# A fused attention, dense layer and expert kernel: softmax by exponentials with sums, fewer float32 products, a reordered first stage

## The chip, the core and the metric

The kernel runs on one core of a Trainium2 chip. The metric is the time of one execution on the device in microseconds (us). Five engines work side by side, each through its own list of instructions in a fixed order: TensorE (PE: matmuls, with its weight loads as PEld), VectorE (DVE), ScalarE (ACT), GpSimd (POOL) and SyncE (SP), whose list issues most DMAs. An instruction starts when the one before it on its engine is through and the semaphores it waits for are set.

## The reference, cut to what matters

```
# 1. chunked attention: 2 batches, 8 heads, 768 tokens, 64 per head; a chunk of 32 queries sees
#    8 memory keys, 16 tokens to the left, its own 32 and 8 to the right (64 keys in all)
scores = scale * q_c @ k_full.T ;  scores -= max(scores)
a = exp(scores) ;  a = a / (sum(a) + 1e-9) ;  attn = a @ v_full
# 2. dense layer on 1536 tokens of 512: weights in float64, 2048 hidden
h = x @ w_in ;  g = where(h > 0, h, exp(min(h, 0)) - 1) ;  x2 = g @ w_out
# 3. 8 experts, 1536 tokens: pick the best, up to `capacity` rows each
logits = x2 @ w_gate ;  e = argmax ;  gate = softmax(logits)[e]
out = gate * (relu(x2 @ w1[e]) @ w2[e])
```

## The kernel before

The 1536 tokens are cut into six tiles of 256 (a tile is a "pair" of two halves u of 128). The 2048 hidden columns are cut into 16 units f of 128. There are 48 steps; a step is one gemm1 (24 matmuls, L409: 128x256 results, float32r) of two (unit, tile) combinations, the activation, and one gemm2 (L464). Steps 0 to 3 take units 0 to 3 on tiles 0 and 1, steps 4 to 15 take one unit on tiles 0 and 1 each, and then each of tiles 2 to 5 has 8 steps. Step s is followed on TensorE by gemm2 of step s-2.

**First stage (tiles 0 and 1).** Its order is a table of tokens, ORDER (L33): a token such as `sc10` is a piece of work for pair 1, half 0, or, such as `cb3`, for unit 3, or, such as `ma4`, for step 4. Every token issues its instructions at once, so the table is the order on every engine.
- Loads on SP: `lu` a unit (two halves of 512 KB, L315), `lk`, `lq`, `lv` (512, 256, 512 KB, L140).
- Attention of a half: `sc` scores into PSUM (64 matmul records, L169), `tm` row maxima (two reduces, L181), `ts` subtraction of the maxima out of PSUM (two, L187), `ex` one exponential of 128x512 on ScalarE (L195), `to` the sums (L204), plus 1e-9 and reciprocal (L205, L206), `di` the product with it on GpSimd (L211), `fl` four transposes, `fc` their copy out of PSUM (L222), `av` the product with v (L233), `xh` and `xl` the high and low parts of the result, which is gemm1's input (L248 on ScalarE, L252 on VectorE).
- Weights come as 64-bit floats; `ca` (ScalarE, L335), `cb`, `cc`, `cd` (VectorE, L339, L343, L349) make float32 of both halves of a unit. `ch`, `cl` (L358, L362) split the w_in half into a rounded part and a rest, `dh`, `dl` the w_out half.
- `ma` gemm1; `mr` three activations (L423 to L425), `mv` two VectorE instructions (L429, L435) that give the layer's g.
- `mb` gemm2. In steps below NWHOLE = 12 (`whole(s)`), g and w_out stay float32 and one product is made: four matmuls of 128x512 (eight records, `ps<-raw,gt`). In the others `mh` (L439, ScalarE) and `ml` (L443, VectorE) split g, and three float32r products are made: 12 matmuls.
- `pw` is a warm-up: two 128x128 matmuls of the identity into PSUM that nobody reads. There are 36, 35 of them ahead of `ma0`.

**Tiles 2 to 5.** A loop over the steps (L914) emits gemm1 of step s+2, its activation and split (`g1b`, L811), gemm2 of step s, and between them background pieces by a table, PLANS: letter A runs the next piece of the next tile's attention (`attention_pair`, up to its next `yield`), R and S the next piece of a finished tile's routing (`route`, L482), which ends in two scatters to DRAM by GpSimd (L573). Routing needs a matmul of the one-hot choices (L539) that waits for VectorE (`oh`, L534).

The experts' part behind it is not touched by the change.

Of the kernel before, what the change touches and what calls it, by code (L numbers as in the profile page):

```python
# [38 lines left out]
def chunk_attention_elu_mlp_moe(  # L39
# [23 lines left out]
    CH, LEFT, RIGHT, WIN = 32, 16, 8, k.shape[-1]  # L63
    NMEM = WIN - LEFT - CH - RIGHT
    KD = DM // P
    NF = FF // P
    NFE = FE // P
    TT = 256
# [8 lines left out]
    w_in_i = w_in.bitcast(I32)  # L77
    w_out_i = w_out.bitcast(I32)
# [46 lines left out]
    cnti = cp_.tile([1, E], I32, name="cnti")  # L125
    turn = cp_.tile([1, E], I32, name="turn")
    lead = cp_.tile([P, 1], F32, name="lead")
    swap = cp_.tile([1, E], F32, name="swap")

    qs = t4([P, 2, KD, P], F32, "q")  # L130
# [22 lines left out]
    class Pair:  # L153
# [24 lines left out]
        def tm(self, u):  # L178
            self.su[u] = mx = ts_([P, 2, KD], F32, "mx")
            for a, sp in enumerate(self.ps["s", u]):  # L180
                nc.vector.tensor_reduce(out=mx[:, a], in_=sp, axis=AX.X, op=ALU.max)  # L181

        def ts(self, u):
            mx, sp = self.su.pop(u), self.ps.pop(("s", u))
            self.a[u] = t2([P, 2, KD, WIN], F32, "a")
            for a in range(2):
# [7 lines left out]
        def ex(self, u):  # L194
            nc.scalar.activation(self.a[u], self.a[u], AF.Exp, scale=ISC)  # L195

        def to(self, u):
            a = self.a[u].rearrange("p a r w -> p (a r) w")
            if self.t == 0 and u == 0:
                nc.vector.memset(a[0:CH, :, L0:M0], 0.0)  # L200
            if self.t == PPB - 1 and u == 1:
                nc.vector.memset(a[P - CH :, :, R0:WIN], 0.0)
            su = ts_([P, 8], F32, "su")
# [3 lines left out]
            self.su[u] = su  # L207

        def di(self, u, eng=nc.gpsimd):
            a, su = self.a[u].rearrange("p a r w -> p (a r) w"), self.su.pop(u)  # L210
# [35 lines left out]
        def xh(self, u):  # L246
            for i, xp in enumerate(self.ps["x", u]):
                nc.scalar.copy(self.part(u, 0, i), xp)  # L248

        def xl(self, u):  # L250
            for i, xp in enumerate(self.ps.pop(("x", u))):
# [6 lines left out]
    def attention_pair(pi):  # L258
        pp = Pair(pi)
        dve = nc.vector.tensor_copy  # L260

        def finish(u):
            pp.av(u)
            pp.xh(u)
            pp.xl(u)
            if pi + 1 < NP:
                load_v(pi + 1, u)

        def soft(u):
# [24 lines left out]
        yield  # L294
        pp.fl(1)
        pp.fc(1, dve)
        yield
        finish(1)
        yield
# [18 lines left out]
    class Unit:  # L318


        def __init__(self, f):
            self.words = []
            for r in raws.pop(f):
                n = 2 // (1 if r.shape[1] == 1024 else 2)
                self.words.append(r.rearrange("p (a c) t -> p a c t", a=n))

        def lows(self):
            return [r[:, :, :, 0] for r in self.words]
# [4 lines left out]
        def ca(self):  # L333
            for hw in self.highs():
                nc.scalar.activation(f32(hw), f32(hw), AF.Copy, scale=float(2.0**-112))  # L335

        def cb(self):
            for lw in self.lows():
                nc.vector.tensor_scalar(out=lw, in0=lw, scalar1=29, scalar2=None, op0=ALU.logical_shift_right)  # L339

        def cc(self):
            for lw, hw in zip(self.lows(), self.highs()):
                nc.vector.scalar_tensor_tensor(  # L343
                    out=lw, in0=hw, scalar=3, in1=lw, op0=ALU.logical_shift_left, op1=ALU.bitwise_or
                )

        def cd(self):
            for lw, hw in zip(self.lows(), self.highs()):
                nc.vector.scalar_tensor_tensor(  # L349
                    out=lw, in0=hw, scalar=-(1 << 31), in1=lw, op0=ALU.bitwise_and, op1=ALU.bitwise_or  # L350
                )
            self.whole = [f32(w) for lw in self.lows() for w in (lw[:, j, :] for j in range(lw.shape[1]))]

        def main(self, i):

            if not hasattr(self, "un"):
                self.un = t8([P, 2, 2, 512], F32R, "un")
            nc.scalar.copy(self.un[:, i, 0, :], self.whole[i])  # L358
# [9 lines left out]
        def ch(self):  # L368
            self.main(0)

        def cl(self):
            self.rest(0)

        def dh(self):
            self.main(1)

        def dl(self):
            self.rest(1)


    NLEAD, NWHOLE = 4, 12
    steps = []
    for ti in (0, 1):
        for f in range(0, NLEAD, 2):
# [401 lines left out]

    if True:
        make_identity(nc, ident)
        nc.gpsimd.memset(ones, 1.0)
        nc.gpsimd.memset(stri, 1.0)  # L790
        nc.gpsimd.affine_select(
# [18 lines left out]

        def g1b(s):  # L811
            if s < len(steps):
                for o in ("mr", "mv") if whole(s) else ("mr", "mv", "mh", "ml"):
                    do(o + str(s))

        def do(tok):
            op, alt = tok[:2], tok.endswith("*")
            n = tok[2:].rstrip("*+-")
            if op == "pw":
                wp = tps([P, P])  # L820
                for _ in range(2):
                    nc.tensor.matmul(wp, ident, ident, start=True, stop=True)
            elif op == "lz":
                i = int(n) * 2 * P
                nc.sync.dma_start(out=disp[i : i + 2 * P, :].rearrange("(a p) c -> p a c", p=P), in_=blank2(ROW))
# [10 lines left out]
            elif op[0] in "cd" and op != "di":  # L836
                f = int(n)
                if f not in units:
                    units[f] = Unit(f)
                getattr(units[f], op)()  # L840
            elif op[0] == "m":
                s = int(n)
                if op == "ma":
# [7 lines left out]
                elif op == "mh":  # L851
                    pend[s] = elu_h(*pend[s])
                elif op == "ml":
                    gts[s] = elu_l(*pend.pop(s))
                elif op == "mb":
                    gemm2(s)
            else:
# [294 lines left out]
```

## Time and profile before

| what | value |
|---|---|
| median of 3 runs | 568.7 us (567.02, 568.7, 571.47) |
| the profiled execution: time, span | 569.6 us, 567.4 us |
| PE busy | 536.4 us (95%) |
| PEld busy | 455.3 us (80%) |
| DVE busy | 360.7 us (64%), 702 instructions |
| ACT busy | 279.3 us (49%), 451 instructions |
| POOL busy | 48.3 us (9%), 58 instructions |

Read it so: TensorE is busy nearly throughout, but its busy time holds warm-ups and stretches at half clock too; the shares are averages over stages with different limits, so each stage is looked at by itself. In the profile, L numbers are lines of this kernel.

### The profile page before, as it was taken

Reading aid. Unit: us, or ns where it says so; the run is one execution under the profiler, and the core shown is the slowest. Engines: PE = TensorE matmul, PEld = TensorE weight load, DVE = VectorE, ACT = ScalarE, POOL = GpSimd, SP = SyncE. Lnnn points to the kernel's source line nnn. Section 1 sums busy time; section 2 is a strip of 40 time slices with the busy share of each in tenths; the row PEclk is TensorE's granted clock in tenths of the full one; section 3 lists DMA queues with packets and bytes.
Section 4 is the critical chain, followed back from the end, with each engine's and each line's share of the span. In section 5 each row is a group of like instructions: output and inputs, shape, how many; then the busy total and the mean of one; then the engine's idle time right before and its main releaser. Section 6 shows DMA issues by size and latency. Waiting matters only on the chain. (4 is left out here: it accounts for less than half of the span.)

```text
span 567.4 us, 11394 instructions
## 1 busy us (share of the span) xinstructions
PE 536.4 (95%) x4598; PEld 455.3 (80%) x4598; DVE 360.7 (64%) x702; ACT 279.3 (49%) x451; POOL 48.3 (9%) x58
## 2 busy tenths in 40 slices
PE   8699999999998799999989999999999899999996
PEld 8687676678887798898879888777887797799894
DVE  4758979787346535678775787762455774684650
ACT  3357555675442443444254435652555664673440
POOL 0200002000001200100100010120001001001001
PEclk9979999999999899999998999999999999999998
DMA  8979322379932211452002276236651894985400
GB/s 334 355 244 386 133 75 70 116 190 266 368 127 76 82 52 62 162 185 94 21 2 76 94 259 223 99 124 209 256 205 36 304 343 153 327 309 158 157 8 25
DMA packets 34725, 95.95 MB, mean 169 GB/s; under 512 B 3424, under 2 KB 3424, under 8 KB 33888
## 3 DMA queue, kind: packets, MB, share of 16 engines
q1 hardware_dynamic: 32496, 88.68, 45.1%
q0 software_dynamic: 2160, 6.31, 2.9%
q8 instruction: 48, 0.79, 0.6%
q14 instruction: 21, 0.17, 0.1%
HBM read 88.67 MB, written 16.55 MB: 185 GB/s over the span
## 5 line engine op out<-in xcount | busy, mean ns | idle before, releaser
L409 PE MATMUL hp<-xt,un 128*128 128x256 f32 x1152 | 151.8, 290 | 1.0 <-DVE th L435 1.0
L409 PEld LDWEIGHTS hp<-xt,un 128*128 128x128 f32 x1152 | 144.9, 194 | 8.1 <-issue 4.2
L464 PE MATMUL ps<-un,gt 128*128 128x512 f32 x432 | 109.6, 403 | 0.7 <-ACT gt L439 0.7
L464 PEld LDWEIGHTS ps<-un,gt 128*128 128x128 f32 x432 | 79.8, 191 | 20.0 <-ACT e L423 1.2
L651 DVE TENSOR_TENSOR eu<-eraw,eu 128x1024 fp32r<-128x1024 f32 x65 | 77.1, 1222 | 19.3 <-ACT eu L650 19.0
L760 PE MATMUL ps<-eu,ht 128*128 128x512 f32 x336 | 83.1, 399 | 1.1 <-DVE eu L651 0.8
L760 PEld LDWEIGHTS ps<-eu,ht 128*128 128x128 f32 x336 | 61.7, 188 | 15.9 <-DVE eu L651 2.1
L429 DVE SCALAR_TENSOR_TENSOR th<-e,th 128x512 f32<-128x512 f32 x48 | 33.6, 700 | 52.7 <-ACT e L425 47.3
L650 ACT CAST eu<-eraw 128x1024 fp32r<-128x1024 f32 x65 | 65.2, 1046 | 0.8 <-ACT os L766 0.8
L697 PE MATMUL hp<-xd,eu 128*128 128x256 f32 x480 | 59.0, 284 | 2.9 <-DVE eu L651 2.1
L697 PEld LDWEIGHTS hp<-xd,eu 128*128 128x128 f32 x480 | 58.1, 192 | 4.3 <-DVE eu L651 2.5
L439 ACT CAST gt<-th 128x512 fp32r<-128x512 f32 x36 | 22.4, 621 | 62.4 <-DVE th L435 62.4
L423 ACT ACTIVATE e<-hp 128x512 f32<-128x512 f32 x48 | 28.5, 595 | 43.1 <-PE hp L409 39.9
L464 PE MATMUL ps<-raw,gt 128*128 128x512 f32 x96 | 45.5, 616 | 0.3 <-DVE gt L435 0.2
L443 DVE TENSOR_TENSOR gt<-th,gt 128x512 fp32r<-128x512 f32 x36 | 24.9, 693 | 23.8 <-ACT gt L439 23.8
L424 ACT ACTIVATE th<-e 128x512 f32<-128x512 f32 x48 | 30.3, 632 | 10.2 <-PE ps L518 5.5
L683 DVE SCALAR_TENSOR_TENSOR ht<-hp,ht 128x512 fp32r<-128x512 f32 x20 | 13.8, 690 | 33.4 <-ACT ht L682 33.4
L464 PEld LDWEIGHTS ps<-raw,gt 128*128 128x128 f32 x96 | 17.2, 188 | 20.4 <-issue 18.6
L722 PE MATMUL hq<-eu,xd 128*128 128x512 f32 x120 | 30.9, 401 | 1.7 <-PE ps L760 1.0
L766 ACT ACTIVATE os<-ps,xg 128x512 f32<-128x512 f32 x15 | 10.3, 687 | 42.2 <-PE ps L760 23.5
L425 ACT ACTIVATE e<-e 128x512 f32<-128x512 f32 x48 | 30.3, 632 | 1.5
L767 POOL DMA_INDIRECT out_dram<-os,xg x15 | 14.6, 975 | 165.8 <-ACT os L766 165.8
(143 smaller groups left out, 564.3 us busy)
## 6 DMA issues: line engine op xcount, KB each, us to landing
eraw<-in_moe_w_dram SPq DMA_DIRECT2D x32, 1024.0 KB, 8.7
raw<-in_moe_w_in_dram SPq DMA_DIRECT2D x15, 512.0 KB, 6.3
raw<-in_moe_w_out_dram SPq DMA_DIRECT2D x15, 512.0 KB, 7.1
disp<-in_blank_dram SPq DMA_DIRECT2D x12, 514.0 KB, 15.6
kt<-in_k_dram SPq DMA_DIRECT2D x12, 512.0 KB, 5.7
v<-in_v_dram SPq DMA_DIRECT2D x12, 512.0 KB, 4.9
wb<-in_gate_rows_dram SPq DMA_DIRECT2D x6, 1024.0 KB, 4.7
xg<-disp SPq DMA_DIRECT2D x8, 514.0 KB, 4.4
```

The lines of the kernel that those rows point to most:

```text
L409: nc.tensor.matmul(hp[:, j, :], units[f].un[:, 0, wp, kk * P : (kk + 1) * P], xts[ti][:, xp, kk, :], start=(n == 0), stop=(n == 3 * KD - 1),)
L423: nc.scalar.activation(e, hv, AF.Relu, scale=-1.0)
L424: nc.scalar.activation(th, e, AF.Tanh, scale=0.5)
L425: nc.scalar.activation(e, e, AF.Exp, scale=-1.0)
L429: nc.vector.scalar_tensor_tensor(out=th, in0=e, scalar=1.0, in1=th, op0=ALU.add, op1=ALU.mult)
L443: nc.vector.tensor_tensor(out=gt[:, 1, :], in0=th, in1=f32(gt[:, 0, :]), op=ALU.subtract)
L464: nc.tensor.matmul(accs[ti][bl], x, w, start=(f == 0 and n == 0), stop=(f == NF - 1 and n == len(passes) - 1),)
L650: nc.scalar.copy(un[:, 0, :], raw)
L651: lows.tensor_tensor(out=un[:, 1, :], in0=raw, in1=f32(un[:, 0, :]), op=ALU.subtract)
L697: nc.tensor.matmul(hp[:, j, :], w1p(kk, wp, f * P, P), xd[xp][:, kk, :], start=(n == 0), stop=(n == 3 * KD - 1),)
L722: nc.tensor.matmul(hp, self.xd[xp][:, kk, self.b0 * P : (self.b0 + 1) * P], w1p(kk, wp, i * 512, 512), start=(n == 0), stop=(n == 3 * KD - 1),
L760: nc.tensor.matmul(acc, hof(f, gp, j), w2p(f, wp), start=(f == 0 and n == 0), stop=(f == NFE - 1 and n == 2))
```

## The change

1. **Softmax.** Except for the first half of a batch and the last (`edge`: 4 of 12 halves), `ts` now makes minus the scaled maxima (one 128x8 VectorE instruction), and `ex` is eight exponentials of 128x64 straight out of PSUM, each with its own maximum as bias and with the sum of its row as a second result. `to` loses the sum over 128x512. The edge halves go on as before.
2. **float32 second products** in steps 0 to 5 only (NWHOLE 12 to 6); steps 6 to 11 get `mh`, `ml` and three float32r products.
3. **Low halves to GpSimd.** A `+` behind a token puts `cl`, `dl` or `ml` on GpSimd (20 in ORDER), and `g1b` does so for every `ml` of tiles 2 to 5. A `*` puts `ch`, `dh`, `xh` or `di` on VectorE (8 in ORDER).
4. **ORDER** is new throughout: pair 0's q and k are loaded ahead of unit 0; 11 warm-ups are left, all ahead of `ma0`, each one matmul of 256 columns instead of two of 128.
5. **Attention pieces** of later tiles: the first is empty, the others come one piece later; `norm(1)` joins the piece of `fl(0)`, `fc(0)`. Their number stays 8.
6. A method `cz` with `signs` is added to `Unit`; no token calls it. One GpSimd memset of 128x1 fills a constant that only `cz` uses.

```
 ORDER = """
-lu0 ca0 cb0 cc0 cd0 ch0 lk00 lq00 pw pw pw pw pw pw pw pw pw pw pw pw pw pw sc00 tm00
+lq00 lk00 pw pw pw pw sc00 tm00 ts00 ex00 lu0 cb0 to00 ca0 lq01 cc0 lk01 pw pw pw pw sc01
...
+        def edge(self, u):
+            return (self.t, u) in ((0, 0), (PPB - 1, 1))
...
+            else:
+                self.su[u] = nm_ = ts_([P, 2, KD], F32, "nm")
+                nc.vector.tensor_scalar(out=nm_, in0=mx, scalar1=-ISC, scalar2=None, op0=ALU.mult)
+
+        def ex(self, u):
+            if self.edge(u):
+                nc.scalar.activation(self.a[u], self.a[u], AF.Exp, scale=ISC)
+                return
...
             for a in range(2):
-                nc.vector.tensor_tensor(
-                    out=self.a[u][:, a],
-                    in0=sp[a],
-                    in1=mx[:, a].unsqueeze(2).to_broadcast([P, KD, WIN]),
-                    op=ALU.subtract,
-                )
+                for r in range(KD):
+                    nc.scalar.activation(
+                        self.a[u][:, a, r, :], sp[a][:, r, :], AF.Exp,
+                        scale=ISC, bias=nm_[:, a, r : r + 1], accum_out=su[:, a, r : r + 1],
+                    )
...
-            nc.vector.tensor_reduce(out=su, in_=a, axis=AX.X, op=ALU.add)
...
     def attention_pair(pi):
...
+        yield
         soft(0)
         yield
         norm(0)
         yield
         soft(1)
         yield
-        norm(1)
-        yield
         pp.fl(0)
         pp.fc(0)
+        norm(1)
         yield
...
-        def rest(self, i):
-            nc.vector.tensor_tensor(
+        def rest(self, i, eng=nc.vector):
+            eng.tensor_tensor(
...
-    NLEAD, NWHOLE = 4, 12
+    NLEAD, NWHOLE = 4, 6
...
-    def elu_l(th, gt):
-        nc.vector.tensor_tensor(out=gt[:, 1, :], in0=th, in1=f32(gt[:, 0, :]), op=ALU.subtract)
+    def elu_l(th, gt, eng):
+        eng.tensor_tensor(out=gt[:, 1, :], in0=th, in1=f32(gt[:, 0, :]), op=ALU.subtract)
...
         def g1b(s):
             if s < len(steps):
-                for o in ("mr", "mv") if whole(s) else ("mr", "mv", "mh", "ml"):
-                    do(o + str(s))
+                for o in ("mr", "mv", "mh", "ml"):
+                    do(o + str(s) + ("+" if o == "ml" else ""))
...
             if op == "pw":
-                wp = tps([P, P])
-                for _ in range(2):
-                    nc.tensor.matmul(wp, ident, ident, start=True, stop=True)
+                wp = tps([P, 2, P])
+                nc.tensor.matmul(wp, ident, ident.unsqueeze(1).to_broadcast([P, 2, P]), start=True, stop=True)
```

How the lists move at three places. First SP's list from its start: q, kt and v are pair loads, raw is a unit (two halves). Before:

```order
L315 DMA raw_108<-in_moe_w_in_dram 128x1024
L315 DMA raw_108<-in_moe_w_out_dram 128x1024
L140 DMA kt_93<-in_k_dram 128x1024
L140 DMA q_92<-in_q_dram 128x512
L315 DMA raw_201<-in_moe_w_in_dram 128x1024
L315 DMA raw_201<-in_moe_w_out_dram 128x1024
L140 DMA q_92<-in_q_dram 128x512
L140 DMA kt_94<-in_k_dram 128x1024
L140 DMA v_95<-in_v_dram 128x1024
```

Changed:

```order
L141 DMA q_93<-in_q_dram 128x512
L141 DMA kt_94<-in_k_dram 128x1024
L337 DMA raw_161<-in_moe_w_in_dram 128x1024
L337 DMA raw_161<-in_moe_w_out_dram 128x1024
L141 DMA q_93<-in_q_dram 128x512
L141 DMA kt_95<-in_k_dram 128x1024
L337 DMA raw_221<-in_moe_w_in_dram 128x1024
L337 DMA raw_221<-in_moe_w_out_dram 128x1024
L141 DMA kt_94<-in_k_dram 128x1024
```

The first scores' operands are now the first two loads, and unit 0 stands behind them; pair 1's first k comes ahead of pair 0's v.

Second, VectorE's list in tile 2, where the routing of tile 0 forms its one-hot choices (`oh`); th is the activation of a step, gt its split. Before:

```order
L429 SCALAR_TENSOR_TENSOR th_1856<-e_1855,th_1856 128x512
L435 SCALAR_TENSOR_TENSOR th_1856<-hp_1787,th_1856 128x512
L443 TENSOR_TENSOR gt_1861<-th_1856,gt_1861 128x512
L528 MAX rmx_1893<-ps_1884 128x8 x2
L530 MAX_INDEX rix_1894<-rmx_1893,ps_1884 128x8 x2
L531 CAST idf_1895<-rix_1894 128x2
L532 TENSOR_SCALAR nmx_1897<-rmx_1893 128x2
L534 TENSOR_SCALAR oh_1896<-iota_e,idf_1895 128x8 x2
```

Changed:

```order
L474 SCALAR_TENSOR_TENSOR th_1813<-e_1812,th_1813 128x512
L480 SCALAR_TENSOR_TENSOR th_1813<-hp_1787,th_1813 128x512
L573 MAX rmx_1850<-ps_1841 128x8 x2
L575 MAX_INDEX rix_1851<-rmx_1850,ps_1841 128x8 x2
L576 CAST idf_1852<-rix_1851 128x2
L577 TENSOR_SCALAR nmx_1854<-rmx_1850 128x2
L579 TENSOR_SCALAR oh_1853<-iota_e,idf_1852 128x8 x2
```

The split's low half (L443) no longer stands between a step's activation and the routing.

Third, GpSimd's list in tile 2: gt rows are the low halves, a rows the attention's products, disp rows the scatters. Before, from the first scatter:

```order
L573 DMA disp<-x_208_1716,rii_1953 3072x514
L211 TENSOR_TENSOR a_1849<-a_1849,su_2014 128x512
L573 DMA disp<-x_208_1716,rii_1953 3072x514
L211 TENSOR_TENSOR a_2056<-a_2056,su_2112 128x512
L573 DMA disp<-x_209_1720,rii_2169 3072x514 x2
```

Changed:

```order
L618 DMA disp<-x_187_1716,rii_1910 3072x514
L488 TENSOR_TENSOR gt_1928<-th_1923,gt_1928 128x512
L233 TENSOR_TENSOR a_2007<-a_2007,su_2014 128x512
L488 TENSOR_TENSOR gt_2050<-th_2045,gt_2050 128x512
L618 DMA disp<-x_187_1716,rii_1910 3072x514
L233 TENSOR_TENSOR a_2108<-a_2108,su_2109 128x512
L618 DMA disp<-x_188_1720,rii_2175 3072x514
L488 TENSOR_TENSOR gt_2186<-th_2181,gt_2186 128x512
L618 DMA disp<-x_188_1720,rii_2175 3072x514
```

Low halves that gemm2 waits for now stand behind scatters and products on this engine.

## Rows read from the trace of the kernel before

**Rows 1.** Windows: stretch, busy us per engine (instructions), granted clock, DMA share, GB/s.

```profile
20.00:30.00 10.00, 4.98 (x199) 4.21 (x199) 5.52 (x14) 3.39 (x7) 2.08 (x2) 0.92 1.01 396
...
44.50:151.50 107.00, 106.08 (x810) 78.66 (x808) 86.34 (x127) 64.44 (x102) 4.46 (x4) 1.00 0.60 191
151.50:200.60 49.10, 44.20 (x524) 39.79 (x524) 25.79 (x85) 19.35 (x40) 6.23 (x6) 0.97 0.34 121
```

**Rows 2.** Timeline of VectorE at the start: start us, us, instruction, [idle before <-releaser].

```profile
5.96 0.70 DVE L339 TENSOR_SCALAR raw<-raw 128x1024 int32<-128x1024 int32 x1 [5.96 <-DMA raw<-in_moe_w_out_dram]
...
9.67 1.23 DVE L349 SCALAR_TENSOR_TENSOR raw<-raw 128x1024 int32<-128x1024 int32 x1
...
11.47 0.74 DVE L187 TENSOR_TENSOR a<-ps,mx 128x256 f32<-128x256 f32 x2
...
13.58 0.69 DVE L204 TENSOR_REDUCE su<-a 128x8 f32<-128x512 f32 x1
```

**Rows 3.** Timeline of TensorE in the first stage.

```profile
33.76 3.80 PE L409 MATMUL hp<-xt,un 128*128 128x256 f32 x24
...
44.49 6.33 PE L409 MATMUL hp<-xt,un 128*128 128x256 f32 x48
...
78.64 3.76 PE L464 MATMUL ps<-raw,gt 128*128 128x512 f32 x8
...
85.11 3.76 PE L464 MATMUL ps<-raw,gt 128*128 128x512 f32 x8
...
136.57 8.56 PE L464 MATMUL ps<-un,gt 128*128 128x512 f32 x36
144.97 5.90 PE L409 MATMUL hp<-xt,un 128*128 128x256 f32 x48
151.53 3.14 PE L409 MATMUL hp<-xt,un 128*128 128x256 f32 x24 [0.66 <-DVE th L435]
```

**Rows 4.** Groups by line and shape: busy us, mean ns of one.

```profile
L429 DVE SCALAR_TENSOR_TENSOR th<-e,th 128x512 f32<-128x512 f32 x48 | 33.6, 700 | 52.7 <-ACT e L425 47.3 <-PE ps L169 3.8 <-issue 1.3
...
L252 DVE TENSOR_TENSOR xt<-ps,xt 128x256 fp32r<-128x256 f32 x24 | 9.0, 416 | 8.8 <-ACT xt L248 8.7
...
L195 ACT ACTIVATE a<-a 128x512 f32<-128x512 f32 x12 | 7.6, 631 | 27.0 <-DVE a L187 27.0
```

**Rows 5.** Timeline of ScalarE: two small exponentials with sums, then the next activation.

```profile
171.20 0.27 ACT L535 ACTIVATE ex<-ps,nmx 128x8 f32<-128x8 f32 x1 [1.04 <-DVE nmx L532]
...
171.70 0.59 ACT L423 ACTIVATE e<-hp 128x512 f32<-128x512 f32 x1
```

**Rows 6.** Timeline of TensorE in tiles 2 and 4.

```profile
171.42 0.18 PE L539 MATMUL ps<-oh,stri 128*128 128x8 bf16 x1 [1.37 <-DVE oh L534]
...
189.27 1.23 PE L233 MATMUL ps<-at,v 64*64 64x32 f32 x64 [1.64 <-ACT at L222]
191.75 0.65 PE L217 MATMUL ps<-ident,a 128*128 128x128 f32 x4 [1.25 <-POOL a L211]
192.16 4.59 PE L464 MATMUL ps<-un,gt 128*128 128x512 f32 x12
...
296.54 1.14 PE L233 MATMUL ps<-at,v 64*64 64x32 f32 x64 [1.77 <-DVE at L222]
```

**Rows 7.** Timeline of VectorE in tile 2: the split's low half.

```profile
169.70 0.69 DVE L443 TENSOR_TENSOR gt<-th,gt 128x512 fp32r<-128x512 f32 x1 [0.69 <-ACT gt L439]
```

**Rows 8.** Timeline: GpSimd's product beside VectorE, and where VectorE reads PSUM.

```profile
84.98 1.83 POOL L211 TENSOR_TENSOR a<-a,su 128x512 f32<-128x512 f32 x1 [57.35 <-DVE su L206]
...
85.95 1.95 DVE L349 SCALAR_TENSOR_TENSOR raw<-raw 128x1024 int32<-128x1024 int32 x1
...
182.90 1.03 POOL L211 TENSOR_TENSOR a<-a,su 128x512 f32<-128x512 f32 x1 [7.55 <-DVE su L206]
```

**Rows 9.** Timeline at the end of tile 5.

```profile
360.52 1.28 POOL L573 DMA_INDIRECT disp<-x,rii  x1 [3.25 <-DMA disp<-x,rii]
...
362.45 3.32 PE L464 MATMUL ps<-un,gt 128*128 128x512 f32 x12 [0.67 <-ACT gt L439]
```

More of the change, by code (lines that the diff above doesn't have):

```diff
@@ L127, in chunk_attention_elu_mlp_moe @@
     lead = cp_.tile([P, 1], F32, name="lead")
+    nought = cp_.tile([P, 1], F32, name="nought")
     swap = cp_.tile([1, E], F32, name="swap")
@@ L181, in tm @@
                 nc.vector.tensor_reduce(out=mx[:, a], in_=sp, axis=AX.X, op=ALU.max)
+        def edge(self, u):
+            return (self.t, u) in ((0, 0), (PPB - 1, 1))
         def ts(self, u):
-            mx, sp = self.su.pop(u), self.ps.pop(("s", u))
+            mx = self.su.pop(u)
+            if self.edge(u):
+                sp = self.ps.pop(("s", u))
+                self.a[u] = t2([P, 2, KD, WIN], F32, "a")
+                for a in range(2):
+                    nc.vector.tensor_tensor(
+                        out=self.a[u][:, a],
+                        in0=sp[a],
+                        in1=mx[:, a].unsqueeze(2).to_broadcast([P, KD, WIN]),
+                        op=ALU.subtract,
+                    )
+            else:
+                self.su[u] = nm_ = ts_([P, 2, KD], F32, "nm")
+                nc.vector.tensor_scalar(out=nm_, in0=mx, scalar1=-ISC, scalar2=None, op0=ALU.mult)
@@ L194, in ex @@
[L194 to L204 removed]
+                for r in range(KD):
+                    nc.scalar.activation(
+                        self.a[u][:, a, r, :], sp[a][:, r, :], AF.Exp,
+                        scale=ISC, bias=nm_[:, a, r : r + 1], accum_out=su[:, a, r : r + 1],
+                    )
@@ new lines, in to @@
+        def to(self, u):
+            if self.edge(u):
+                a = self.a[u].rearrange("p a r w -> p (a r) w")
+                if u == 0:
+                    nc.vector.memset(a[0:CH, :, L0:M0], 0.0)
+                else:
+                    nc.vector.memset(a[P - CH :, :, R0:WIN], 0.0)
+                self.su[u] = ts_([P, 2, KD], F32, "su")
+                nc.vector.tensor_reduce(out=self.su[u].rearrange("p a r -> p (a r)"), in_=a, axis=AX.X, op=ALU.add)
+            su = self.su[u]
@@ L244, in part, with xh @@
             return x.rearrange("p (g i) x -> p i g x", i=2)[:, i]
-        def xh(self, u):
+        def xh(self, u, cp=nc.scalar.copy):
             for i, xp in enumerate(self.ps["x", u]):
-                nc.scalar.copy(self.part(u, 0, i), xp)
+                cp(self.part(u, 0, i), xp)
         def xl(self, u):
@@ L335, in ca, with cz @@
                 nc.scalar.activation(f32(hw), f32(hw), AF.Copy, scale=float(2.0**-112))
-        def cb(self):
-            for lw in self.lows():
-                nc.vector.tensor_scalar(out=lw, in0=lw, scalar1=29, scalar2=None, op0=ALU.logical_shift_right)
+        def cz(self):
+            x = t4([P, 1024], F32, "sign")
+            self.signs = []
+            for i, hw in enumerate(self.highs()):
+                n = hw.shape[1]
+                to = x[:, i * 512 : i * 512 + n * 512].rearrange("p (a c) -> p a c", a=n)
+                nc.scalar.activation(to, f32(hw), AF.Identity, scale=float(2.0**-100), bias=nought)
+                self.signs.append(to.bitcast(I32))
+        def cb(self):
+            for i, lw in enumerate(self.lows()):
+                if self.signs:
+                    nc.vector.scalar_tensor_tensor(
+                        out=lw, in0=lw, scalar=29, in1=self.signs[i],
+                        op0=ALU.logical_shift_right, op1=ALU.bitwise_or,
+                    )
+                else:
+                    nc.vector.tensor_scalar(out=lw, in0=lw, scalar1=29, scalar2=None, op0=ALU.logical_shift_right)
         def cc(self):
@@ L366, in rest, with ch, cl, dh @@
                 self.words = self.whole = None
[L368 to L378, printed above, removed]
-    NLEAD, NWHOLE = 4, 12
+        def ch(self, **kw):
+            self.main(0, **kw)
+        def cl(self, **kw):
+            self.rest(0, **kw)
+        def dh(self, **kw):
+            self.main(1, **kw)
+        def dl(self, **kw):
+            self.rest(1, **kw)
+    NLEAD, NWHOLE = 4, 6
     steps = []
@@ L839, in do @@
                     units[f] = Unit(f)
-                getattr(units[f], op)()
+                kw = {}
+                if alt:
+                    kw = {"cp": nc.vector.tensor_copy}
+                elif tok.endswith("+"):
+                    kw = {"eng": nc.gpsimd}
+                getattr(units[f], op)(**kw)
             elif op[0] == "m":
```

25 lines of the change are left out of this document (17 added, 8 removed).

## The prediction, made before the changed kernel ran

> **What bounds the kernel now.** I read the busy shares first: TensorE is busy 95%, so time can only be won by giving it less to do, by letting it start its real work earlier, or by closing its waits. The windows by stage say which of these is open where [rows 1]. From 44.5 to 151.5 us TensorE is busy 106.1 of 107.0 us at full clock (1.00): there only less work helps, and VectorE, busy 86 us of the same stretch, is not far behind. From 151.5 to 200.6 us (tile 2) it is busy 44.2 of 49.1. Before 44.5 its busy time is largely warm-ups; the DMAs run flat out (share 1.01 at 396 GB/s between 20 and 30 us) and the clock is 0.92 there. The timeline of TensorE gives the landmarks of the first stage [rows 3]: the first gemm1 begins at 33.8 us, that of step 2 at about 47.7 (44.5 plus half of the 6.3 of two), tile 2's first at 151.5. So I price four things: when step 2's gemm1 can begin, what lies between it and tile 2, the waits in tiles 2 to 5, and the end of tile 5. What follows the dense layer is the same program, and I carry it over unchanged.
>
> **Second products.** One step with float32 takes 6.47 us from gemm2 to gemm2 (78.64 to 85.11). With three float32r products it is 2.80 for gemm2 (36 matmuls, 136.57 to 144.97, three steps) and 2.95 for gemm1 (48 in 5.90, two steps), together 5.75 [rows 3]. Difference 0.72, six steps: **-4.3 us** of a TensorE that is full there. For it, six more `mh` and `ml` run: 3 to 4 us on ScalarE, which is busy 64 of 107, and on GpSimd or VectorE.
>
> **The early start.** From row 1 of VectorE: 1 MB, the first load, has landed at 5.96 us [rows 2]. At 396 GB/s the 0.75 MB of q and k that now lead land about 0.7 us sooner, near 5.2, and scores need some 0.9: VectorE can start attention at 6.1. From there I count VectorE's list up to the last input of step 2's gemm1 (pair 1's last `xl`), with row durations less the 0.05 to 0.08 by which instructions of one engine overlap in the timeline. Conversion of a unit: 0.62 + 1.17 + 1.17 = 2.96, five units, 14.8 [rows 2]. Row maxima of five halves, 0.70 each for a pair (the subtraction pair took 0.74): 3.5. One edge subtraction 0.70 and three small ones of 0.18: 1.2. Sums: one in the old way 1.2 (0.69 plus small ones), three new ones 0.36 each: 2.3. Four `xl` of two, 0.68: 2.7 each 0.42 less the overlap [rows 4]. One activation pair 1.4 0.70 each [rows 4]. Moved to VectorE by a `*`: 2.0. Sum 27.9. Walking the list against ScalarE, GpSimd and the landings (512 KB each 1.3 us at that rate, units 0 to 3 by 24 us), I find VectorE idle 4.9 us, nearly all while eight exponentials run. So step 2's gemm1 begins at 6.1 + 27.9 + 4.9 = 38.9, say 39.7 with TensorE's own list: **-8.0 us** against 47.7. The 24 warm-ups that go lay ahead of that point and cost nothing by themselves; what they kept up, the clock, is rival 2.
>
> The eight exponentials themselves: two small ones with sums took 0.50 us from start to start [rows 5], 0.25 each for 8 elements; from 0.27 at 8 to 0.63 at 512 elements [rows 4] 56 more cost some 0.04, an estimate, at most 0.1. So 2.3 to 2.8 us a half instead of 0.63, while VectorE loses 0.74 + 0.69 and gains 0.18. I take 2.5. In the dense part this runs beside ScalarE's idle time; on the chain of a half it adds about 0.5 us.
>
> **From step 2 to tile 2** it was 103.8 us. Off go 4.3, and 0.8 for one half's scores that now come earlier. Against it stands a collision. The product on GpSimd took 1.03 us where VectorE read PSUM, but 1.83 beside VectorE's conversions, and a conversion 1.95 instead of 1.23 [rows 2, 8]. Twenty low halves and five products now run there in the first stage. I take +2.0 us of waits for it (bounds: 0 if VectorE keeps ahead, 6.6 as in rival 1). **-3.1.**
>
> The Trainium skill has a rule on this (SBUF — State Buffer, Who interferes with whom): a VectorE instruction with two SBUF inputs and a GpSimd instruction that reads SBUF use one shared port pair as an exclusive lock, and the second to issue waits until the first is through. By that rule a low half moved to GpSimd beside a busy VectorE gives VectorE back nothing; the two lengthened rows agree with it, and rival 1 is what would follow.
>
> **Tile 2.** TensorE waited 1.37 for the one-hot choices, 1.64 for `fc`'s copy, 1.25 for the product, and the gemm2 behind them took 4.59 instead of 2.80 [rows 3, 6]: the clock had fallen to its half level, 1.2 GHz, after these waits. Together 6.1. The choices were late because VectorE stood 0.69 us waiting for ScalarE's rounding and then made the low half, 0.69, ahead of them [rows 7]; both are gone. In my walk the new pieces put two gemm1, a gemm2 and the second half's scores between `di` and `fl` of the first half, and `fc` is late by 0.5 only, behind eight exponentials. **-5.6**; bounds: 0 if the exponentials hold up `fc` and the clock as before, -6.1.
>
> **Tiles 3 to 5.** The pattern repeats in tile 4: a second wait of 1.4 for the choices, one of 1.77 for a copy on VectorE [rows 6], a second slow matmul group behind it. VectorE now reaches both 1.3 us sooner, so the first goes and the other shrinks; I take **-3.3**, bounds 0 and -5. The `ml` of these steps has time: ready some 5.5 us after its gemm1, wanted two gemm2 and two gemm1 later, 11.5. Only the last two steps have no gemm1 behind them: there TensorE already waited 0.67 for the split [rows 9], and GpSimd needs 1.03 to 1.83 instead of 0.69: **+1.0** (0.3 to 2).
>
> **Sum.** -8.0 - 3.1 - 5.6 - 3.3 + 1.0 = -19.0, from the profiled execution's 569.6 us: 550.6. That execution lies 0.9 above the median of 568.7, so I forecast **550 us** for the median.
>
> **Rival 1: VectorE becomes the pace.** From step 2's gemm1 to that of step 7 my count gives VectorE 34.3 us and TensorE 32.8, so there is no room. About nine GpSimd instructions fall in this stretch; each holds VectorE up by 0.72 (1.95 less 1.23) [rows 2, 8]: 6.6 us instead of the 2.0 allowed, and about 2 of tile 4's gain go the same way. Against it: some of these meet VectorE at PSUM reads or waits. Time 550 + 4.6 + 2 = 556.6. Chance 0.18.
>
> **Rival 2: the early start is lost to the clock.** With 11 warm-ups TensorE is mostly idle up to step 0's gemm1, at about 24 us; even with 35 the clock was 0.92, and the first gemm1 took 3.80 us [rows 1, 3]. If the half level lasts through three gemm1 and a gemm2 (some 13 us at full), and half of that is hidden by VectorE's list, step 2 begins 6 to 7 us later: 557. Chance 0.12.
>
> **Rival 3: GpSimd's list paces tiles 2 to 5, slower than before.** A low half stands behind scatters; one waited 3.25 us for the scatter before it and took 1.28 [rows 9]. A tile has 8 low halves, 2 products and 2 to 4 scatters: at 1.83, 1.83 and 4.5 us that is 27 to 36 us of the 46 that eight steps take. If instructions there cost half as much again it passes 46; then each of 32 steps waits, at 0.85 us 27 us in all: 577. Against it: 10 us of room, and two steps of lead. Chance 0.06.
>
> **Chances and range.** The forecast has 0.64. The range must take in rivals 1 and 2 and the bounds: below, all of the collision's 2.0, another 0.5 in tile 2 and 1.7 in tile 4, and some more if step 2 starts with less idle time on VectorE: 540. Above, rival 2 with part of rival 1: 561. Less than 2 in 10 is left out. A change of 1% (5.7 us) is about what a measurement of this kernel can tell from none. Faster by more: 0.88 (the forecast and rivals 1 and 2, less their overlap beyond 563); within 1%: 0.05; slower: 0.07 (rival 3 and a little).
>
> **What would show it.** Step 0's gemm1 near 24 to 26 us and step 2's near 40; tile 2's first gemm1 near 140 instead of 151.5; gemm2 of steps 6 to 11 as 12 matmuls in 2.8 us; exponentials of 128x64 every 0.3 us; no wait on `oh` in tiles 2 and 4, and no slow matmuls behind it; tile 2 some 43 us long. Wrong would be: TensorE waiting for VectorE's `th` or `gt` in steps 3 to 8 (rival 1), a granted clock near half up to 40 us with gemm1 of 5 to 6 us (rival 2), or TensorE waiting for GpSimd's `gt` in tiles 2 to 5 (rival 3).

## The result, and the profile after

The changed kernel took **552.1 us** (median of 548.2 to 555.1) beside 568.7 before: ratio 0.970, 95% interval 0.963 to 0.977. On a second chip the same program took 555.8 (553.7 to 559.4) beside 569.7: 0.977 (0.970 to 0.983). So it is 14 to 17 us faster; I had forecast 550 within 540 to 561.

The profiled execution took 555.1 us (span 553.4; before 569.6 and 567.4). Its windows by stage, in the columns of [rows 1]:

```profile
10.00:20.00 10.00, 7.02 (x201) 5.60 (x202) 8.38 (x15) 6.27 (x23) 4.40 (x4) 0.59 1.03 416
20.00:30.00 10.00, 8.79 (x227) 7.12 (x225) 8.71 (x17) 8.66 (x39) 3.76 (x3) 0.90 1.02 397
30.00:42.91 12.91, 11.90 (x164) 9.78 (x165) 10.38 (x19) 7.02 (x13) 1.67 (x2) 0.74 1.03 415
42.91:142.00 99.09, 97.83 (x746) 79.55 (x745) 82.71 (x112) 64.22 (x115) 25.97 (x20) 1.00 0.64 207
142.00:187.14 45.14, 43.54 (x527) 39.49 (x525) 22.07 (x77) 21.00 (x54) 14.25 (x12) 0.96 0.22 71
...
345.55:553.40 207.85, 191.11 (x1115) 163.65 (x1113) 106.42 (x140) 101.44 (x142) 20.05 (x20) 0.99 0.52 184
```

Step 2's gemm1 begins at 42.9 us (before 47.8), tile 2's first at 142.0 (151.5), the experts' part at 345.6 (365.6). (What the prediction and this text call tile 2's first gemm1 is that of step 18, the first that the loop emits; steps 16 and 17, also of tile 2, run ahead of it in both kernels, so the comparison holds.) The dense part ends 20.1 us earlier; the experts' part, which the change does not touch, took 207.9 us instead of 201.8 and gives 6 of that back. Its window before:

```profile
365.61:567.40 201.79, 189.22 (x1115) 162.43 (x1113) 106.70 (x140) 101.46 (x142) 19.16 (x18) 0.99 0.54 188
```

TensorE's timeline of the changed kernel, to be read beside [rows 3] (up to 104.13 us) and [rows 6, 9] (the rest):

```profile
24.34 0.39 PE L454 MATMUL hp<-xt,un 128*128 128x256 f32 x1
24.89 3.02 PE L454 MATMUL hp<-xt,un 128*128 128x256 f32 x23 [0.16 <-DVE xt L274]
...
31.01 0.63 PE L239 MATMUL ps<-ident,a 128*128 128x128 f32 x4 [1.72 <-DVE a L233]
...
34.97 4.93 PE L454 MATMUL hp<-xt,un 128*128 128x256 f32 x24
39.74 3.76 PE L509 MATMUL ps<-raw,gt 128*128 128x512 f32 x8
42.91 3.45 PE L454 MATMUL hp<-xt,un 128*128 128x256 f32 x24
...
98.46 2.96 PE L509 MATMUL ps<-un,gt 128*128 128x512 f32 x12
101.26 3.03 PE L454 MATMUL hp<-xt,un 128*128 128x256 f32 x24
104.13 2.94 PE L509 MATMUL ps<-un,gt 128*128 128x512 f32 x12
...
177.09 1.14 PE L255 MATMUL ps<-at,v 64*64 64x32 f32 x64 [1.55 <-ACT at L244]
178.27 0.66 PE L239 MATMUL ps<-ident,a 128*128 128x128 f32 x4
178.69 4.60 PE L509 MATMUL ps<-un,gt 128*128 128x512 f32 x12
...
250.22 0.17 PE L587 MATMUL ps<-oh,stri 128*128 128x8 bf16 x1 [0.88 <-DVE oh L579]
...
343.12 2.60 PE L509 MATMUL ps<-un,gt 128*128 128x512 f32 x10 [0.63 <-POOL gt L488]
```

In tile 2 one wait is left, for `fc`'s copy, and behind it the slow gemm2 (4.60 instead of 2.96). Of the choices' waits one of 0.88 in tile 4 remains. The copy is late because of what stands ahead of it on ScalarE:

```profile
172.65 1.29 POOL L488 TENSOR_TENSOR gt<-th,gt 128x512 fp32r<-128x512 f32 x1 [2.26 <-ACT gt L484]
...
172.76 1.21 DVE L202 TENSOR_SCALAR nm<-mx 128x8 f32<-128x8 f32 x1
...
174.09 0.31 ACT L213 ACTIVATE a<-ps,nm 128x64 f32<-128x64 f32 x1 [1.58 <-DVE nm L202]
174.30 0.19 ACT L213 ACTIVATION_READ_ACCUMULATOR a<-ps,nm 128x1 f32 x1
174.39 0.31 ACT L213 ACTIVATE a<-ps,nm 128x64 f32<-128x64 f32 x1
...
176.41 0.62 ACT L244 COPY at<-ps 128x512 f32<-128x512 f32 x1
```

These are lines of GpSimd, VectorE and ScalarE: the eight exponentials of the second half start every 0.29 us (2.3 us in all; the forecast said 2.3 to 2.8) and the first half's copy stands behind them; and they began late, since the 8-element scaling of the maxima took 1.21 us beside a low half on GpSimd.

### The profile page after: what moved, and what is told of

Same layout as the page of the kernel before. It is cut to its first block, busy times and chain, and to the rows that moved or that the text cites. A ratio compares the mean times of both kernels' runs of the same rounds, so it can differ in the third digit from the quotient of the medians.

```text
span 553.4 us, 11372 instructions
## 1 busy us (share of the span) xinstructions
PE 523.3 (95%) x4500; PEld 448.5 (81%) x4500; DVE 348.1 (63%) x651; ACT 293.5 (53%) x569; POOL 120.1 (22%) x108
## 5 line engine op out<-in xcount | busy, mean ns | idle before, releaser
L509 PE MATMUL ps<-un,gt 128*128 128x512 f32 x504 | 127.2, 401 | 1.4 <-POOL gt L488 1.3
L509 PEld LDWEIGHTS ps<-un,gt 128*128 128x128 f32 x504 | 92.7, 191 | 22.5 <-POOL gt L488 2.4
L805 PE MATMUL ps<-eu,ht 128*128 128x512 f32 x336 | 84.7, 404 | 6.2 <-ACT eu L695 3.4
L805 PEld LDWEIGHTS ps<-eu,ht 128*128 128x128 f32 x336 | 62.9, 191 | 21.5 <-issue 5.7
L488 POOL TENSOR_TENSOR gt<-th,gt 128x512 fp32r<-128x512 f32 x33 | 45.8, 1388 | 127.9 <-ACT gt L484 127.8
L484 ACT CAST gt<-th 128x512 fp32r<-128x512 f32 x42 | 26.1, 620 | 73.3 <-DVE th L480 73.3
L407 POOL TENSOR_TENSOR un<-raw,un 128x512 fp32r<-128x512 f32 x16 | 23.6, 1481 | 56.7 <-ACT un L403 40.5
L480 DVE SCALAR_TENSOR_TENSOR th<-hp,th 128x512 f32<-128x512 f32 x42 | 29.1, 692 | 4.0 <-DVE th L474 0.5
```

The lines of the kernel that those rows point to most:

```text
L480: nc.vector.scalar_tensor_tensor(out=to, in0=hv, scalar=0.0, in1=th0, op0=ALU.max, op1=ALU.subtract)
L488: eng.tensor_tensor(out=gt[:, 1, :], in0=th, in1=f32(gt[:, 0, :]), op=ALU.subtract)
L509: nc.tensor.matmul(accs[ti][bl], x, w, start=(f == 0 and n == 0), stop=(f == NF - 1 and n == len(passes) - 1),)
L805: nc.tensor.matmul(acc, hof(f, gp, j), w2p(f, wp), start=(f == 0 and n == 0), stop=(f == NFE - 1 and n == 2))
```

## The experiments

Beside each median, "start" is tile 2's first gemm1 in the trace, "tiles" the time from there to the experts' part, "experts" the rest. Before: 151.5, 214.1, 201.8. Changed: 142.0, 203.5, 207.9. These three come from one profiled execution of each kernel, which can lie some us from the median.

**The six steps' products alone, first try** (kernel before):

```
-NLEAD, NWHOLE = 4, 12
+NLEAD, NWHOLE = 4, 6
-... mv6 ... mb6 dh6 ... dl6        (and 7 to 11)
+... mv6 mh6 ml6 ... dh6 dl6 mb6
```

> The kernel before with one part of the change: steps 6 to 11 make three float32r products (NWHOLE 6), their rounding and low half on ScalarE and VectorE. My step: six steps at 0.72 us less on a TensorE that is full there, -4.3 us, so about 564.4, and tile 2's first gemm1 at about 147.2 instead of 151.5. Rival (VectorE is nearly as full): its six more low halves (3.7 us) eat it, -1 to -2 us, 567, with TensorE waiting for gt or un.

610.4 us, ratio 1.072 (1.070 to 1.074). I had put `dh6` straight ahead of `mb6`, and so behind the next step's activations in ScalarE's list, which wait for that step's gemm1: gemm2 could no longer run beside them, and TensorE waited 4.8 to 7.4 us in front of three gemm2. That says nothing on the products.

**The table of before in the changed kernel, with the same misplaced tokens:**

> The changed kernel with the first stage's table of before (with the rounding and low half of steps 6 to 11 added), all else as changed. If the early start and the reordering are worth what the change's trace shows (-9.5 us at tile 2's first gemm1, of which 4.3 are the products), the first gemm1 of tile 2 comes at 147 and the whole at about 557 (552 + 5). Rival: the lighter softmax by itself brings most of the early start (VectorE has 1.2 us less per half): step 2's gemm1 already 2 to 3 us earlier, the whole at 554. In tiles 2 to 5 both expect the gains of the change (some 10 us from tile 2's first gemm1 to the end of step 47), since these parts are kept.

596.0 us, 1.045 (1.041 to 1.049), spoiled in the same steps. Two things can be read outside of them: step 2's gemm1 came at 48.3, so the lighter softmax alone brings nothing of the early start (that rival falls); and tiles took 203.3 us, so the gain there does not hang on the first stage.

**The products alone, mended:** each `dh dl` pair of units 6 to 11 stands behind a step's `ml` or a unit's `cl`, ahead of the next step's activations.

> As the first try of this part (six more steps with three float32r products in the kernel before), but with the w_out halves of units 6 to 11 rounded and split ahead of the next step's activations on ScalarE and VectorE, not behind them: in the first try gemm2 of steps 6 to 11 waited up to 7.4 us for un, because its rounding stood behind the next step's gemm1 in ScalarE's list. With that mended my step should hold: six times 0.72 less, -4.3 us, 565, tile 2's first gemm1 at 147.2. Rival: VectorE has no room for six more low halves and six earlier ones (7.4 us): -2 to +3 us, with waits for un or th in steps 8 to 12.

580.3 us, 1.021 (1.016 to 1.027). The rival came true, and worse than I had put it. Up to step 7 nothing is lost (-1.1 us); then TensorE waits for VectorE and ScalarE, three of its waits:

```profile
89.45 4.03 PE L409 MATMUL hp<-xt,un 128*128 128x256 f32 x22 [2.26 <-DVE un L362]
...
100.75 0.49 PE L464 MATMUL ps<-un,gt 128*128 128x512 f32 x1 [1.20 <-ACT un L358]
...
106.44 4.83 PE L464 MATMUL ps<-un,gt 128*128 128x512 f32 x12 [2.08 <-ACT gt L439]
```

Between 84 and 110 us VectorE is busy 23.0 of 26, and in the kernel before it was busy 23.1 in the same stretch, where TensorE did not wait at all: it had little room for more. Tile 2 starts at 157.3, 5.8 us later than before. In the old table the six steps cost time in both placings that were tried; a better one may exist.

**All but the table:** the changed kernel with this mended table.

> The changed kernel with the first stage's table of before, with the mended places for the six steps' halves; all else as changed. If the reordering is worth what the traces showed (5.2 of the 9.5 us by which tile 2 starts earlier), tile 2's first gemm1 comes at 147 and the whole is 5 us above the changed kernel, 557 to 561. From tile 2's first gemm1 to step 47 it takes 190.5 us as in the changed kernel (200.7 before). Rival (order and products only work together, the old table leaves VectorE no room): tile 2 starts at 150 or later, the whole 564 or more.

562.6 us, 0.988 (0.983 to 0.994). Start 156.3, tiles 201.8. As to tile 2's start the rival came true again: the new table, with its marks, is worth 12 to 14 us at tile 2's start (142.0, and 144.2 in the second trace of the changed kernel), not 5.

**The first stage's low halves on VectorE:**

```
-... cl1+ ... cl0+ ... cl2+ ...
+... cl1  ... cl0  ... cl2  ...     (20 tokens; the expectation counted 18)
```

> The changed kernel with the 18 low halves that the first stage's table puts on GpSimd moved to VectorE (0.6 us each, 11 us more on an engine that is busy 82.7 of 99.1 us). Relief theory: VectorE becomes late, TensorE waits for un and th in steps 2 to 10, tile 2 starts 4 to 8 us later, 557 to 560. Lock theory (each low half on GpSimd holds VectorE up by about 0.7 us as it is): within 1.5 us of the change, 552, and VectorE's conversions come down from 1.32 to 1.23 us.

560.4 us, 0.987 (0.983 to 0.990). The relief theory came true: tile 2 starts at 151.25, 9.3 us later than in the first trace of the changed kernel and 7.1 later than in the second. That is still 5 us ahead of the old table (156.3), so the new order gives something without its `+` marks too. Step 2's gemm1 comes at 47.1 instead of 42.9, and a later step waits 4.0:

```profile
28.07 4.88 PE L454 MATMUL hp<-xt,un 128*128 128x256 f32 x22 [3.35 <-DVE un L407]
...
38.76 0.78 PE L255 MATMUL ps<-at,v 64*64 64x32 f32 x37 [2.18 <-issue]
...
127.23 4.31 PE L454 MATMUL hp<-xt,un 128*128 128x256 f32 x22 [4.00 <-DVE un L407]
```

`issue` means that TensorE waited for nothing that the profile shows; that line is no work of VectorE, see the run with the moved code. What VectorE paid shows in the windows up to tile 2's first gemm1, this kernel first (VectorE is the third busy time), then the changed one:

```profile
0.00:151.25 151.25, 133.60 (x1414) 108.40 (x1415) 116.61 (x187) 88.61 (x190) 8.35 (x19) 0.93 0.70 244
```

```profile
0.00:142.00 142.00, 131.95 (x1414) 106.73 (x1415) 113.11 (x167) 89.24 (x190) 37.26 (x39) 0.94 0.74 260
```

Twenty instructions of 0.7 us, 14 us, left VectorE, and it is busy only 3.5 us less: the others grew (the scaling of the maxima from 0.18 to 0.63 us, mean of four; `cb` from 0.75 to 0.82; `cd` from 1.22 to 1.32). The Trainium skill (SBUF — State Buffer, Who interferes with whom) says that a VectorE instruction with two SBUF inputs contends with a GpSimd instruction that reads SBUF, under an exclusive lock; `cd`, which has two, agrees. The scaling and `cb` have one SBUF input and grew too. If each low half on GpSimd held VectorE up for as long as it would have taken there, the move would return nothing; measured, a quarter came back. The time gained at tile 2's start is larger than that: with the low halves on VectorE, TensorE waits for them (`un`, 3.35 and 4.00 us above).

**Low halves of g in tiles 2 to 5 on VectorE:** `do(o + str(s))` in `g1b`, without the `"+"` for `ml`.

> The changed kernel with the low halves of g in tiles 2 to 5 on VectorE as before. My theory: they put the one-hot choices late; TensorE's wait for oh (1.4 us each in tiles 2 and 4) comes back, and with it a slow gemm2 or two; less 0.6 us in the last two steps: +2 to +5 us, about 555. Rival 1 (the shared port makes VectorE pay for GpSimd's low halves anyway): 0 within 1 us. Rival 2: GpSimd's low halves cost more than they give, -1 to -3 us.

559.0 us, 0.982 (0.980 to 0.983). My theory was right in kind and too small: tiles 210.8, 7.2 us more. The wait for `oh` is back in tile 4 (2.24 instead of 0.88) and not in tile 2; the first wait below is in the changed kernel too (1.55):

```profile
178.31 1.13 PE L255 MATMUL ps<-at,v 64*64 64x32 f32 x64 [1.67 <-ACT at L244]
...
253.75 0.17 PE L584 MATMUL ps<-oh,stri 128*128 128x8 bf16 x1 [2.24 <-DVE oh L579]
286.27 1.14 PE L255 MATMUL ps<-at,v 64*64 64x32 f32 x64 [0.96 <-DVE at L244]
308.90 0.17 PE L651 MATMUL ps<-cum,ones 128*128 128x8 bf16 x1 [1.31 <-DVE cum L596]
```

**The pieces of attention as before** (the `yield` ahead of `soft(0)` gone, `norm(1)` ahead of `fl(0)` as a piece of its own):

> The changed kernel with the pieces of attention in tiles 2 to 5 cut as before (softmax of the first half starts one place earlier, transposes and copy of the first half after the second half's product). My theory: the wait for GpSimd's product in front of the transposes comes back in tiles 2 and 4, 1.25 us each, with a slow gemm2 behind the one of tile 2: +2 to +4 us. Rival (only the order of low halves and choices matters there): within 1 us.

563.2 us, 0.988 (0.983 to 0.994), 7.3 us above the changed kernel on this chip, and so more than forecast. In the trace tiles are 213.4, 9.9 us more; that execution took 568.8, 5.6 above the median, so 9.9 may be too much. In tile 2:

```profile
181.34 1.14 PE L255 MATMUL ps<-at,v 64*64 64x32 f32 x64 [3.55 <-ACT at L244]
184.52 1.11 PE L239 MATMUL ps<-ident,a 128*128 128x128 f32 x4 [2.04 <-POOL a L233]
```

Eight exponentials in the old pieces hold up the copy by 3.55. So GpSimd's low halves (7.2) and the new pieces (9.9) do not add up: in these traces the low halves alone keep 0.7 of the 10.5, the pieces alone 3.3. Both were run with the eight exponentials, so the old pieces with the old softmax are not shown.

**The softmax of before** (`edge` true for every half, the zeroing only where `edge` was true):

> The changed kernel with the softmax of before in all halves (two subtractions, one exponential, one sum over 128x512), order and all else kept. My count: VectorE gets 1.2 us more for each of the three light halves ahead of step 2's gemm1, but gets the exponentials 1.7 us sooner each; the two cancel: step 2's gemm1 within 1 us, the whole +1 to +2 us, 553 to 554. In tile 2 the wait for the copy of the first half (1.55 us) goes, since the eight exponentials no longer stand ahead of it, and VectorE's 1.2 us more comes back as a wait for oh. Rival (VectorE's load decides, as where the first stage's low halves went back to it: +7.6 us for 11 us more on VectorE): +3 to +5 us.

550.2 us (549.1 to 553.9), 0.966 (0.961 to 0.970), beside 555.8 of the changed kernel on this chip. Start 143.9, 1.9 later than in the first trace of the changed kernel and 0.3 earlier than in the second; tiles 200.3, 3.2 and 2.6 us less, nearly all of it in tile 2; the experts' part took 208.0. I had missed the sign: the eight exponentials do not pay here. Of the 5.6 us between the medians the traces show 2.5. Tile 2 without them:

```profile
177.33 1.14 PE L255 MATMUL ps<-at,v 64*64 64x32 f32 x64
178.44 0.66 PE L239 MATMUL ps<-ident,a 128*128 128x128 f32 x4
178.85 3.05 PE L509 MATMUL ps<-un,gt 128*128 128x512 f32 x12
```

No wait, and no slow gemm2. VectorE's longer subtractions and sums cost nothing there.

**The changed kernel again:**

> The changed kernel as it is, as the measure for the others of this chip: 552 us (548 to 555). In its first trace TensorE stood still at two places of the experts' part, 3.2 us (546 matmuls behind its start) and 1.9 us (921 behind), and that part took 207.9 us instead of 201.8. If the place is set by the program, both stalls are there again within 0.5 us; if by what the DMAs happen to do, other places and other sizes.

555.8 us. Experts 207.6. Both stalls are at the same matmuls as in the first trace, and smaller by 0.6 and 0.5 us. The first block below is of this run, the second of the first trace:

```profile
448.28 7.32 PE L805 MATMUL ps<-eu,ht 128*128 128x512 f32 x24 [2.59 <-ACT eu L695]
...
515.78 4.22 PE L805 MATMUL ps<-eu,ht 128*128 128x512 f32 x17 [1.37 <-issue]
```

```profile
446.76 5.83 PE L805 MATMUL ps<-eu,ht 128*128 128x512 f32 x24 [3.23 <-ACT eu L695]
...
512.96 5.77 PE L805 MATMUL ps<-eu,ht 128*128 128x512 f32 x17 [1.91 <-issue]
```

The profile names ScalarE's `eu` for the first, but on the weight loads the same idle time reads `[3.40 <-issue]`: nothing it knows was late. The DMA queues in that stretch (443.5 to 446.9 us; packets, MB, share of 16 engines) hold a transfer of another kind:

```profile
q1 hardware_dynamic: 522, 1.28, 100.0%
q8 instruction: 1, 0.02, 1.7%
```

**The code moved:** 32 matmuls more ahead of the first scores.

> The changed kernel with 32 matmuls of 16 columns whose result nobody reads, put where TensorE waits for the first k (8.1 to 10.3 us), so that everything behind keeps its work and stands 64 instructions later in TensorE's list. The trace has transfers of 16 KB on a queue of kind 'instruction', one for each 250 or so instructions of TensorE, and one of them lies inside each of the two stalls of the experts' part (at 444.2 and 510.5 us). If TensorE stood still there for its own instructions, the stalls leave their places (546 and 921 matmuls behind the start of that part) and the part's length changes by 1 to 6 us, while step 2 to tile 5 stay within 1 us. Rival (an input was late there): the 3.2 us stall stays at its place.

558.8 us, 0.982 (0.977 to 0.988). My filler was too dear: each matmul is two records with a weight load each (so 128 instructions, not 64), and they took 10.6 us, far more than the 2.2 in which TensorE waits there:

```profile
5.15 10.56 PE L871 MATMUL ps<-ident 128*128 128x16 f32 x64
15.64 1.19 PE L170 MATMUL ps<-kt,q 64*32 64x64 f32 x64
```

Scores are 10 us late and tile 2 starts 7.7 us late. But tiles took 203.5 as in the changed kernel, and experts **203.4** instead of 207.6 to 207.9: neither stall is at its place, and the longest idle times left are two of 1.6 us at other matmuls. The same work, moved in TensorE's list, lost them.

Moving the code also moved everything in time, but the other traces settle that. Count TensorE's matmul records ahead of the experts' part. Where there are as many as in the changed kernel (its two traces, the two with low halves on VectorE, the pieces of before), idle time stands at the 546th matmul of that part (1.2 to 3.2 us) and at the 921st or 922nd (0.9 to 2.0), and the part takes 205.8 to 210.8, whether it begins at 345.6 or at 356.2 us. Where there are 24 to 98 more (the kernel before, both runs with the table of before, this run and the two below), neither place stalls, and the part takes 201.8 to 203.7. The two runs of the products alone have 122 more, with their weight loads 244 instructions, and both stalls are back, at the 546th and at the 924th or 925th (parts of 205.4 and 208.8). The softmax of before is the one that does not fit: as many matmuls as the changed kernel, but five more waits in TensorE's list, and idle times at the 602nd and 918th.

**A version put together from the runs, and the same with half the filler:** softmax of before, `ml` of steps 46 and 47 on VectorE, and in place of the four warm-ups ahead of `sc01` 64 (or 32) matmuls of 8 columns in bfloat16.

> A version put together from the runs: the changed kernel with the softmax of before (550.2 beside 555.8 on one chip), the low halves of the last two steps on VectorE, and 64 matmuls of 8 columns in place of four warm-ups (112 instructions more in TensorE's list, near the 128 of the run with the moved code, in which the experts' part took 203.4 us instead of 207.6 to 208). Expected: -0.6 us for the last two steps, -4 us for the experts' part if the stalls leave, 545 to 546. Rival 1: the stalls only change places, 549. Rival 2: without these warm-ups the clock keeps TensorE back up to step 2's gemm1, 1 to 3 us later.

> The same with 32 of the small matmuls (48 instructions more instead of 112). If the stalls of the experts' part come from where TensorE's blocks of instructions end, this version differs from the other in that part by 1 to 5 us, either way, and their dense parts agree within 1 us. If they come from inputs or from the DMAs' load, both take the same.

**545.1 us** (544.9 to 545.2), 0.958 (0.954 to 0.963), and 547.3 (546.8 to 551.3), 0.964 (0.958 to 0.970). The first beats both kernels. Start 141.5 and 141.2, tiles 200.0 and 200.7, experts 201.9 and 203.4: their dense parts agree, the experts' parts differ by 1.5, and the second kernel has a stall of 2.33 at a new place (403.6 us) with an instruction transfer at 401.3. Rival 2 of the first expectation fell: with the small matmuls in place of four warm-ups step 2's gemm1 came at 41.0, earlier than 42.9.

## Why the prediction was right, and where it was not

The forecast case came true, but its terms moved against each other, so that the total came out within 2 us is in part luck. Term by term in the traces (first, and second execution of the changed kernel):

- Early start: forecast -8.0, measured -4.9 and -5.1. VectorE's list was about right: its last input was done at 40.5 us, forecast 38.9. What failed is "39.7 with TensorE's own list": TensorE had waited 1.72 us for VectorE's product (31.01), and behind that wait its granted clock was 0.66 and then 0.57, the lower level (1.2 GHz) for most of the time. The two products with v took 3.4 us there and gemm1 of step 1 4.8, together some 3 us more than the same groups take at full clock later in this trace; so gemm2 of step 0 ran only from 39.74 to 42.9. That is a piece of rival 2, about half its price.
- Step 2 to tile 2: forecast -3.1, measured -4.7 and -2.3. The rows of a step came as priced (2.80 and 2.87 us from start to start at 98.46, 101.26 and 104.13, 5.7 a step). But "six steps at 0.72" was put down as a gain of its own, and by itself it was none: in the old table, as I placed them, the same six steps cost 5.8 us. The saving came only with the room that the new table makes. I had the sum about right with wrong parts.
- The collision on GpSimd and VectorE, +2.0: from step 2 to tile 2 TensorE's waits for GpSimd's `gt` and `un` sum to 1.1 us (0.65 and 0.48). Rival 1's lengthening is real, but the low halves on GpSimd are worth 7 to 9 us all the same.
- Tiles 2 to 5 with the end: forecast -7.9 (5.6 and 3.3 off, 1.0 on), measured -10.5 and -11.2. By tiles, in the first trace: -3.9 in tile 2, nothing in tile 3, -4.6 in tile 4, -2.0 in tile 5. In tile 2 the exponentials' delay was sized 0.5 and is 1.55 with a slow gemm2 behind. Tile 4 gave more than its 3.3. In tile 5 the last two steps' cost did not come (the wait is 0.63 where it was 0.67 [rows 9]), and a wait of the kernel before that the sum had left out is gone (1.17 for `cum`, below). Rival 3 did not show: GpSimd is busy 120 of 553 us.
- Experts: forecast 0, measured +6.1 and +5.8. This is the step that failed most. "The same program, carried over unchanged" left out that its place in TensorE's list changes. The two stalls make up 5.1 and 4.0 us of it.

Dense part forecast -19.0, measured -20.1 and -18.5; with the experts' part -14.0 and -12.7 against one profile of before, and -16.6 and -13.9 by the medians.

The lines to these readings: VectorE's last input and the granted clock of the early start in the changed kernel (the clock is the last column but two), and the wait in tile 5 of the kernel before.

```profile
39.77 0.75 DVE L274 TENSOR_TENSOR xt<-ps,xt 128x256 fp32r<-128x256 f32 x2
```

```profile
31.00:34.97 3.97, 3.96 (x133) 3.65 (x133) 3.57 (x8) 2.34 (x4) 1.30 (x1) 0.66 1.02 411
34.97:39.74 4.77, 4.77 (x27) 4.77 (x26) 4.21 (x6) 1.73 (x3) 0.00 (x0) 0.57 1.03 412
```

```profile
320.61 0.17 PE L606 MATMUL ps<-cum,ones 128*128 128x8 bf16 x1 [1.17 <-DVE cum L551]
```

Shown by runs: the worth of the table, the pieces, GpSimd's low halves, the loss by the eight exponentials in tile 2, and that the two stalls go with the code's place (one trace, with the softmax of before, fits only in part). Open: how the table's gain divides between the loads, the warm-ups and the order; and why instructions come late at just those places. That they do come late there is an inference from the `issue` and the transfers. The part has branches at run time, and the DMAs are busy there (the 100.0% above); heavy traffic alone does not do it, for in the kernel before a transfer at 465.75 us fell into as much (share 1.01) and TensorE was busy throughout. No run separated these.

## What to carry to other kernels

Price a change's parts together where one makes room for the other: the same six steps lost 5.8 us in one table and fit in another, and two cures did not add up. Eight small exponentials with sums free VectorE but put 2.3 us ahead of everything behind them on ScalarE; look there for a copy that TensorE needs. When a part that is not touched becomes slower, look for idle time put down to `issue`, and move the code before explaining it.

## What the hardware showed that I had not expected

- Instructions come by the same DMA engines during the run: 46 transfers of 16 KB on a queue of kind `instruction` in the changed kernel. In the dense part there is about one per 250 instructions of TensorE, so I take them for TensorE's; 122 matmuls with their weight loads, close to one transfer, brought the two stalls back. Most transfers cost nothing. Near some that fell into heavy DMA traffic TensorE stood idle 1.4 to 3.2 us, at the start (3.15 us in the kernel before, in front of 29.0 us; 2.18 with the first stage's low halves on VectorE) and in the experts' part.
- A VectorE instruction on 128x8 elements took 1.21 us beside one of GpSimd, and ended with it; with GpSimd's low halves gone from the first stage the same instruction took 0.18 there.
- An exponential with a sum is two instructions on ScalarE, 0.31 and 0.19 us, overlapped to 0.29 from one to the next.
